# The down product of a bilinear gated unit, on one Trainium2 core: eight block products replaced by seven over 1024 tokens

## The chip, the core and the metric

The kernel is one program on one NeuronCore of a Trainium2 chip. The metric is the device time of one execution in microseconds (us). Engines are called by the profile's names: PE (TensorE, matmuls), PEld (its weight loads), DVE (VectorE), ACT (ScalarE), POOL (GpSimd) and SP (SyncE, which issues most DMAs). Each engine works through its own instructions strictly in the order in which the kernel was written, and waits at an instruction until what it reads and overwrites is free; so the order on each engine is as important as the amount of work.

## The reference

Cut to the part that the change touches. Sizes: S = 2048 tokens, D = 640, F = 1536, one batch, float32.

```python
x = A_u
sa, ca, ga, sb, cb, gb = ...                 # six rows of D from silu(c) @ w_mod
h = layernorm(x) * (1 + ca) + sa
x = x + ga * long_convolution(h, ...)        # the first two thirds of the time
h = layernorm(x) * (1 + cb) + sb
g = h @ w_gate                               # D -> F
u = h @ w_up                                 # D -> F
x = x + gb * ((g * u) @ w_down)              # F -> D: the down product
```

## The kernel before

The convolution fills the first 530 us or so of the span and is left as it is. Then comes the gated unit, in two halves of 1024 tokens, each of two blocks of 512 tokens. Every half has a stage that makes g * u for twelve blocks of 128 of F (the up stage), and a stage that multiplies it by w_down (the down stage).

**Precision by splitting.** A float32 product is made of three faster ones: each operand is split into hi and lo (`hilo`, L1020: ACT writes hi, DVE subtracts to get lo), and PE adds up hi x hi, lo x hi and hi x lo (`prod`, L1053). So every operand that PE reads costs one ACT and one DVE instruction first. Both are recorded under the helper's lines: L229 for ACT, L1022 for DVE.

**The up stage** (loop over f, L1565 on) makes, for each block f of F, products `y_1`, `z_1`, `y_2`, `y_3`, `z_2` (and `x_1`, `x_2` for a block three steps ahead); DVE adds them out of PSUM (L1394 in `y_1`, L1406 in `y_2`, L1425 in `y_3`, L1414 in `z_2`), multiplies for the first token block (L1419), and POOL adds and multiplies for the second (L1408, L1426). The results are tiles `a` of 128 x 512: the transposed g * u, by block of F. The products lie in six PSUM banks used in turn (`pa`, L1061), so a product can start only when the sum that was made six products earlier has been read out.

**The down stage** (L1606 on) runs over token blocks T and over f. `d_prep` (L1431) splits one tile `a` (512 columns) and one block of 128 rows of w_down (640 columns, tiles wga, wsgh, wsgl); `down` (L1446) then runs 24 matmuls: 4 groups of 128 tokens x 3 products x 2 column ranges, 384 and 256 wide. That is 48 steps in all, 24 for each half, 1152 matmuls. `d_prep` runs three steps ahead (LEAD). After twelve steps `fin` (L1467) adds the sum to the residual x on DVE (L1471, L1474) and stores it. w_down is multiplied by gb on POOL during the first up stage (`fold`, L1491, product at L1503) and kept in a DRAM tile, wdg.

**What the first down stage carries besides.** The second half's tokens need a layer norm first: `stats` (L1509: 20 DVE statistics instructions, L1105, for each block, then a chain of short ones, L1091 and L277 to L284, with a square root on ACT between them), `head_i` (four ACT instructions of 640 columns), and `tokens2` (four PE transposes, an ACT scaling, a split). A table, LATER (L1519), says at which step each is written; before, they stand at steps 1 to 4 of the first token block and at steps 0 to 9 of the second.

## Time and profile before

| | us |
|---|---|
| runs | 1008.56, 1013.97, 1013.34 (median 1013.34) |
| span of the profiled execution | 1012.8 |
| first up stage until first down matmul | to 683.47 |
| first down stage until the second half's first product | 683.47 to 775.79 |
| second half's first products and up stage | 775.79 to 923.95 |
| second down stage | 923.95 to about 1008.6 |
| last sums and stores | to 1012.8 |

The profiled execution has a span of 1012.8 us; the device time of an execution adds what lies around its span, and the profile does not give it for this one. Stage borders are read in the timeline of PE. The profile is read by three things: the busy time of each engine in a stretch of time, what an engine waited for, and the timeline of one engine, where a square bracket behind a row gives the idle time before it and who ended it.

### The profile page before, as it was taken

The numbers are of one execution on the slowest core, as the hardware profiler recorded it, in microseconds if no ns is written. First come the engines' busy times: TensorE is split into PE (matmuls) and PEld (weight loads), VectorE is DVE, ScalarE is ACT, GpSimd is POOL, SyncE is SP. The second block draws the span as 40 slices with busy tenths as digits, with TensorE's granted clock in tenths as the row PEclk, the third lists the DMA queues.
The fourth block names the chain that finished last, engine by engine and source line by source line (L and its number), as shares of the span: only waits on it lengthen the run. The fifth ranks groups of instructions, "written<-read, shape, count | busy, mean of one in ns | idle before, by whom it ended". The sixth has DMA issues, their size and how long they took to land. (4 is left out here: it accounts for less than half of the span.)

```text
span 1012.8 us, 26818 instructions
## 1 busy us (share of the span) xinstructions
PE 897.8 (89%) x11192; PEld 732.0 (72%) x11192; DVE 765.8 (76%) x1389; ACT 574.4 (57%) x1049; POOL 572.4 (57%) x423
## 2 busy tenths in 40 slices
PE   4864798799789689988888999999999999999998
PEld 3653566576576467666746788889998888889998
DVE  8698578987989987893977977787576787768452
ACT  4759999987888897872437322234464422224331
POOL 4976899799869989950035576661112354452000
PEclk9876799999979989999999999999999999999999
DMA  7654665454445553558673444524644422221341
GB/s 243 236 140 151 235 230 151 161 163 130 142 129 159 168 150 104 179 170 283 209 208 94 151 134 136 191 109 130 211 157 160 152 79 82 86 67 54 103 157 52
DMA packets 147817, 153.16 MB, mean 151 GB/s; under 512 B 9200, under 2 KB 125424, under 8 KB 146288
## 3 DMA queue, kind: packets, MB, share of 16 engines
q1 hardware_dynamic: 145968, 148.43, 46.4%
q10 hardware_dynamic: 1728, 3.02, 0.8%
q8 instruction: 88, 1.44, 0.6%
...
HBM read 110.45 MB, written 40.96 MB: 150 GB/s over the span
## 5 line engine op out<-in xcount | busy, mean ns | idle before, releaser
L708 POOL TENSOR_TENSOR EQ<-LQ,RH 128x1536 f32<-128x1536 f32 x40 | 124.2, 3106 | 23.0 <-DVE QtB L765 22.8
L229 ACT ACTIVATE z<-pa 128x512 f32<-128x512 f32 x24 | 14.4, 599 | 168.6 <-PE pa L1057 120.5
L1022 DVE TENSOR_TENSOR wsgl<-wga,wsgh 128x640 fp32r<-128x640 f32 x72 | 67.9, 947 | 45.7 <-ACT wsgh L229 45.6
L229 ACT ACTIVATE wsgh<-wga 128x640 fp32r<-128x640 f32 x72 | 52.6, 732 | 66.7 <-PE pa L1459 42.7
L1408 POOL TENSOR_TENSOR z<-z,s 128x512 f32<-128x512 f32 x24 | 33.6, 1400 | 92.9 <-DVE s L1407 92.9
L1034 POOL TENSOR_TENSOR tf<-wur,wgb 128x256 f32<-128x256 f32 x24 | 18.9, 785 | 93.1 <-DVE wtl L1022 57.7
L1459 PE MATMUL pa<-wsgh,sh 128*128 128x384 f32 (+1 forms) x304 | 69.7, 310 | 0.0
L1459 PE MATMUL pa<-wsgl,sh 128*128 128x384 f32 (+1 forms) x304 | 69.2, 309 | 0.0
L1459 PE MATMUL pa<-wsgh,sl 128*128 128x384 f32 (+1 forms) x304 | 69.1, 309 | 0.0
L708 POOL TENSOR_TENSOR EP<-LP,RH 128x768 f32<-128x768 f32 x40 | 66.1, 1652 | 0.0
L708 POOL TENSOR_TENSOR Pha<-LH,DH 128x1536 int32<-128x1536 int32 (+1 forms) x21 | 62.5, 2974 | 3.7 <-ACT trb L229 3.3
L708 POOL TENSOR_TENSOR Phb<-LH,DH 128x1536 int32<-128x1536 int32 x20 | 62.3, 3115 | 3.1 <-ACT tra L229 3.1
L1022 DVE TENSOR_TENSOR wtl<-tf,wth 128x256 fp32r<-128x256 f32 (+1 forms) x72 | 60.1, 861 | 0.0
L820 PE MATMUL kg<-QtB,PtB 64*32 64x64 f32 x2560 | 48.2, 227 | 4.9 <-DVE QtB L764 4.9
L820 PEld LDWEIGHTS kg<-QtB,PtB 64*32 64x32 f32 x2560 | 41.0, 113 | 12.8 <-DVE QtB L764 6.2
L1406 DVE TENSOR_TENSOR s<-pa,s 128x512 f32<-128x512 f32 x24 | 16.6, 690 | 44.6 <-PE pa L1057 39.6
L1057 PE MATMUL pa<-sh,wtl 128*128 128x512 f32 x144 | 45.1, 395 | 4.2 <-DVE wtl L1022 4.2
L1459 PEld LDWEIGHTS pa<-wsgh,sh 128*128 128x128 f32 x304 | 46.6, 188 | 0.0
L1459 PEld LDWEIGHTS pa<-wsgh,sl 128*128 128x128 f32 x304 | 46.6, 188 | 0.0
L1459 PEld LDWEIGHTS pa<-wsgl,sh 128*128 128x128 f32 x304 | 46.6, 188 | 0.0
L1057 PE MATMUL pa<-sh,wth 128*128 128x512 f32 x144 | 44.7, 391 | 0.0
L1057 PE MATMUL pa<-sl,wth 128*128 128x512 f32 x144 | 44.5, 390 | 0.0
(576 smaller groups left out, 2953.2 us busy)
## 6 DMA issues: line engine op xcount, KB each, us to landing
...
```

The lines of the kernel that those rows point to most:

```text
L229: return S.activation(o, i, f, **kw)
L708: G.tensor_tensor(o.rearrange("p x (h l) -> p x h l", l=8), lo.unsqueeze(2).to_broadcast([P, rows, nh, 8]), hi.rearrange("p h x -> p x h") ...
L820: PE.matmul(kg[j * 32 : j * 32 + 32, dd, :], PtB[lo : lo + 64, c, r, :], QtB[lo : lo + 64, c, r, :], start=False, stop=dd == 7 and c == 1, ...
L1022: V.tensor_tensor(lo, v, hi, op=OP.subtract)
L1034: G.tensor_tensor(t[:, 0:2], u[:, 0:2], g[:, 0:2], op=OP.subtract)
L1057: PE.matmul(ps, w[a][:, k], x[b][:, l], start=n == 0 and m == 0, stop=n == 2 and m == len(ks) - 1)
L1406: V.tensor_tensor(S67[i], ps, S6[i], op=OP.add)
L1408: G.tensor_tensor(ZT[i], ZT[i], S67[i], op=OP.add)
L1459: PE.matmul(ACC[tb][t][c], x[:, ts], w[:, cs], start=st, stop=f == NF - 1 and n == 2 and (c == 0 or t % 2 == 1))
```

## The change

The down product of a half is now taken as one product of 1024 x 1536 by 1536 x 640, cut into 2 x 2 blocks on each side: tokens 512 and 512, F 768 and 768, D 320 and 320. Instead of the eight block products it makes seven (Winograd's form of Strassen's method), of sums and differences of blocks. A product runs over six blocks of F, two at a time, so it has three steps; a half has 21 steps q = 0 to 20, each with 24 matmuls of 320 columns (4 groups of 128 tokens x 2 blocks of F x 3 products), 1008 in all.

- The tiles `a` are held in pairs of two blocks of F, 128 x 1024 (`AV`; AV[0..5] first token block, AV[6..11] second). `d_prep(h, q)` splits one such pair (1024 columns) and one 128 x 640 tile of weights for each step, two steps ahead. In the first half the lo part of steps 8, 10, 12, 14 and 16 is made on POOL instead of DVE (`hilo` has an engine as argument).
- Block sums of the left side: `half_sum` (m = 0, 1, 2; written behind steps 0, 1, 2) is POOL add, DVE subtract, POOL subtract, each of 1024 columns (lines 1460, 1461, 1462 of the new kernel); `half_sum4` (behind steps 7, 8, 9) is a POOL subtract (line 1465). Sum and operands are read by steps 6 to 17.
- Block sums of w_down: `fold` in the first up stage keeps its twelve products with gb and adds twelve subtractions of 640 columns on POOL, and writes seven blocks for each part of F to wdg.
- Results: a product lies in four PSUM banks, two products in turn in eight banks. `fin` behind every third step adds a product to the residual blocks: product 0 is copied out by ACT (four copies of 320) and added on POOL, products 1 to 6 are added on DVE straight from PSUM (4 or 8 instructions of 320, line 1543), and the sums that several results share are added on POOL behind that (8 for product 2, 4 for product 5).
- The second half's token work moves: `stats` of both blocks is written in the last two steps of the first up stage, each behind `d_prep` of that step; `head_i` behind steps 1 and 2, the transposes behind steps 7, 10 and 13, the sums for the second up stage behind 15 and 16.

The diff, cut to its core:

```diff
+    DW, NP, NQ = D // 2, 7, 21
...
-        PAIRS += [("d", 2 * h + T, 2 * p) for T in range(2) for p in range(NF // 2)]
+        PAIRS += [("d", h, q) for q in range(0, NQ, 2)]
...
-    def hilo(hi, lo, v):
+    def hilo(hi, lo, v, e=None):
         act(hi, v)
-        V.tensor_tensor(lo, v, hi, op=OP.subtract)
+        (e or V).tensor_tensor(lo, v, hi, op=OP.subtract)
...
+    AHEAD = 4
+    PROD = (0, 3, 0, 6, 9, None, 3)
+    AH, WD2, AR, S1, XR, ACC, U = {}, {}, {}, {}, {}, {}, {}
...
+    def half_sum(h, m):
+
+        S1[m] = two(mk(("wth", "wth", "wtl")[m], [P, 8, P], F32R, 2).bitcast(F32))
+        x11, x21, x22 = AV[m], AV[6 + m], AV[9 + m]
+        G.tensor_tensor(S1[m], x21, x22, op=OP.add)
+        V.tensor_tensor(x21, x11, x21, op=OP.subtract)
+        G.tensor_tensor(x11, S1[m], x11, op=OP.subtract)
+
+    def half_sum4(h, m):
+        G.tensor_tensor(AV[3 + m], AV[3 + m], AV[m], op=OP.subtract)
+
+    def slot_of(q):
+
+        if q < 2:
+            if q == 0:
+                AR[0] = [mk(n, [P, NB, 512], F32R) for n in ("hh1", "hl1")]
+            return [t[:, 2 * q : 2 * q + 2] for t in AR[0]]
+        if q < 18:
+            if q == 2:
+                AR[0] = [mk(n, [P, 9, 512], F32R) for n in SX]
+            i = 2 * ((q - 2) % 4)
+            return [t[:, i : i + 2] for t in AR[0]]
+        return [two(mk(n, [P, 8, P], F32R, 2)) for n in ("wth", "wtl")]
+
+    def d_prep(h, q):
+
+        p, m = divmod(q, 3)
+        w = WR.pop(("d", h, q))
+        v = S1.pop(m) if PROD[p] is None else AV[PROD[p] + m]
+        if q < 20:
+            ah, al = slot_of(q)
+            hilo(ah, al, v, G if h == 0 and q in (8, 10, 12, 14, 16) else None)
...
+        WD2[h, q] = mk("wsgh", [P, D], F32R, 4), mk("wsgl", [P, D], F32R, 4)
+        hilo(*WD2[h, q], w)
+        if q % 2 or q == NQ - 1:
+            used(1)
...
+    def bank(p, t):
+        j = 4 * (p % 2) + t
+        return pa(ACC["b"] + j) if j < 6 else pg(j - 6)
+
+    def down(h, q):
+
+        p, m = divmod(q, 3)
+        if q == 0:
+            ACC["b"] = BANK[0]
+            BANK[0] += 4
+        if m == 0:
+            ACC[p] = [bank(p, t) for t in range(4)]
+        x, (dh, dl) = AH.pop((h, q)), WD2.pop((h, q))
+        last = h == 1 and q == NQ - 1
+        for a, b in [(t, j) for t in range(4) for j in range(2)] if last else [(t, j) for j in range(2) for t in range(4)]:
+            ts, ws = slice(a * P, a * P + P), slice(b * DW, b * DW + DW)
+            ah, al = x[b]
+            for n, (l, r) in enumerate(((ah, dh), (al, dh), (ah, dl))):
+                PE.matmul(ACC[p][a][:, :DW], l[:, ts], r[:, ws], start=m == 0 and b == 0 and n == 0, stop=m == 2 and b == 1 and n == 2)
...
+        def add(e, x, y):
+            for t in range(4):
+                e.tensor_tensor(x[t], y[t], x[t], op=OP.add)
+
+        if p == 0:
+            for t in range(4):
+                act(u[t], ps[t])
+            add(G, x11, u)
+        if p == 1:
+            add(V, x11, ps)
+            store(h, 0, 0)
+        if p == 2:
+            add(V, u, ps)
+            add(G, x21, u)
+            add(G, x22, u)
+        if p == 3:
+            add(V, x21, ps)
+            add(V, x22, ps)
+        if p == 4:
+            add(V, x21, ps)
+            store(h, 1, 0)
+        if p == 5:
+            add(V, u, ps)
+            add(V, x22, ps)
+            add(G, x12, u)
+            store(h, 1, 1)
+        if p == 6 and h == 0:
+            add(V, x12, ps)
+            store(h, 0, 1)
+        elif p == 6:
+            for t in range(4):
+                V.tensor_tensor(x12[t], ps[t], x12[t], op=OP.add)
+                (SY, S)[t % 2].dma_start(rows_of(h, 0, 1, outv)[:, t], x12[t])
...
+        if p < 2:
+            for k in ((0, 1, 2), (3,))[p]:
+                G.tensor_tensor(x[:, k], x[:, k], gbr, op=OP.mult)
+        if p == 1:
+            G.tensor_tensor(t1, b12, b11, op=OP.subtract)
+            G.tensor_tensor(t3, b22, b12, op=OP.subtract)
+        if p == 2:
+            G.tensor_tensor(t2, b22, t1, op=OP.subtract)
+            G.tensor_tensor(t4, b21, t2, op=OP.subtract)
+            rs = slice(2 * r, 2 * r + 2)
+            for c, b in ((0, b11), (1, b21), (6, b22)):
+                SY.dma_start(wdg[:, c, rs], b)
+            SY.dma_start(wdg[:, 2:6, rs].rearrange("p c j d -> p c (j d)"), FT[1])
+            if r < 2:
+                fold_l(r + 1)
...
+    LATER = {1: [(head_i, 2)], 2: [(head_i, 3)], 3: [(raw_u, NF)], 5: [(raw_u, NF + 1)],
+             7: [(new_h,)] + [(tokens2, 2, 0, k, False, (1, i)) for i, k in enumerate((0, 2, 1, 3))],
+             10: [(tokens2, 2, 0, 4, False, (0, 0))] + [(tokens2, 3, 1, k, False, (0, i + 1)) for i, k in enumerate((0, 2, 1))],
+             13: [(tokens2, 3, 1, 3, False, (1, 0)), (tokens2, 3, 1, 4, False, (1, 1))],
...
+    BOTH = {0: [(half_sum, 0), (res_l, 0, 0)], 1: [(half_sum, 1), (res_l, 1, 0)], 2: [(half_sum, 2)], 6: [(res_l, 1, 1)],
+            7: [(half_sum4, 0)], 8: [(half_sum4, 1)], 9: [(half_sum4, 2)], 15: [(res_l, 0, 1)]}
...
-                d_prep(2 * half, f - NF + 2)
-        for T in range(2):
-            tb = 2 * half + T
-            h2 = tb + 2 if half == 0 else None
-            for f in range(NF):
-                for n in (2, 3) if T == f == 0 else (f + LEAD,):
-                    if n < NF:
-                        d_prep(tb, n)
-                    elif T == 0:
-                        d_prep(tb + 1, n - NF)
-                    elif h2:
-                        split_g(n)
-                down(tb, f)
-                if f == NF - 1:
-                    fin(tb)
-                for g_, *a_ in LATER.get((T, f), ()) if h2 else ():
-                    g_(*a_)
+                d_prep(half, f - NF + 2)
+                if half == 0:
+                    for i_ in (0, 2):
+                        stats(f - NF + 4, i_)
+        for q in range(NQ):
+            if q + 2 < NQ:
+                d_prep(half, q + 2)
+            down(half, q)
+            if q % 3 == 2:
+                fin(half, q // 3)
+            for g_, *a_ in BOTH.get(q, ()):
+                g_(half, *a_)
+            for g_, *a_ in LATER.get(q, ()) if half == 0 else ():
+                g_(*a_)
```

**DVE, end of the first up stage.** Rows from the adds of the last-but-one block of F to the start of the down stage; `a`, `s`, `z`, `e` are the tiles of the up stage, `sl` or `hl` the lo part of a left operand, `wsgl` that of the weights. Before:

```order
L1022 TENSOR_TENSOR e<-a_7635,e 128x512
L1022 TENSOR_TENSOR wsgl<-wga,wsgh 128x640
L1394 TENSOR_TENSOR s_8894<-pa_8887,e 128x512
L1406 TENSOR_TENSOR s_8915<-pa_8908,s_8894 128x512
L1407 TENSOR_TENSOR s_8894<-z,s_8894 128x512
L1425 TENSOR_TENSOR s_8915<-pa_8919,s_8915 128x512
L1414 TENSOR_TENSOR s_8894<-pa_8931,s_8894 128x512
L1419 TENSOR_TENSOR a_8700<-a_8700,s_8894 128x512
L1022 TENSOR_TENSOR e<-a_7636,e 128x512
L1022 TENSOR_TENSOR wsgl<-wga,wsgh 128x640
L1022 TENSOR_TENSOR sl<-a_7637,sh 128x512
```

After (BN_STATS and what follows it are the layer norm's statistics):

```order
L1028 TENSOR_TENSOR hl_8889<-a_7630,hh_8888 128x1024
L1028 TENSOR_TENSOR wsgl<-wga,wsgh 128x640
L1111 BN_STATS st_8896<-xb_8814 128x6 x20
L1097 BN_AGGR mv_8917<-st_8896 128x2 x4
L277 TENSOR_SCALAR hr_8920<-mv_8917 128x4
L279 RECIPROCAL hr_8918<-hr_8921 128x4
L280 TENSOR_TENSOR hr_8921<-hr_8918 128x4
L281 TENSOR_TENSOR hr_8921<-hr_8921,hr_8920 128x4
L282 TENSOR_SCALAR hr_8921<-hr_8921 128x4
L283 TENSOR_TENSOR hr_8918<-hr_8918,hr_8921 128x4
L284 SCALAR_TENSOR_TENSOR hr_8919<-mv_8917,hr_8918 128x4
L1415 TENSOR_TENSOR s_8941<-pa_8934,e 128x512
```

The statistics of both token blocks now stand on DVE between the splits of steps 0, 1 and 2, the first of them ahead of the last block's adds out of PSUM, which begin with L1415 (L1394 of before).

**DVE, first steps of the down stage, after.** The rows from the split of step 2 on; L1461 is the middle instruction of `half_sum`:

```order
L1028 TENSOR_TENSOR sl<-a_7940,sh 128x1024
L1028 TENSOR_TENSOR wsgl<-wga,wsgh 128x640
L1461 TENSOR_TENSOR a_7635<-a_7630,a_7635 128x1024
L1028 TENSOR_TENSOR sl<-a_8162,sh 128x1024
L1028 TENSOR_TENSOR wsgl<-wga,wsgh 128x640
L1461 TENSOR_TENSOR a_8059<-a_7631,a_8059 128x1024
L1028 TENSOR_TENSOR sl<-a_8379,sh 128x1024
L1028 TENSOR_TENSOR wsgl<-wga,wsgh 128x640
L1461 TENSOR_TENSOR a_8282<-a_7940,a_8282 128x1024
L1028 TENSOR_TENSOR sl<-a_8602,sh 128x1024
L1028 TENSOR_TENSOR wsgl<-wga,wsgh 128x640
```

Each difference of blocks stands ahead of the split of the next step: L1461 for m = 2 is ahead of the split of step 5.

**POOL, the same place, after.** L1460 and L1462 are the first and last instruction of `half_sum`, L1543 the adds of product 0 to the residual:

```order
L1429 TENSOR_TENSOR z<-z,s_8962 128x512
L1447 TENSOR_TENSOR a_7636<-s_8962,z 128x512
L1460 TENSOR_TENSOR wth<-a_7635,a_8504 128x1024
L1462 TENSOR_TENSOR a_7630<-wth,a_7630 128x1024
L1460 TENSOR_TENSOR wth<-a_8059,a_8717 128x1024
L1462 TENSOR_TENSOR a_7631<-wth,a_7631 128x1024
L1543 TENSOR_TENSOR hh_9076<-s_9150,hh_9076 128x320
L1543 TENSOR_TENSOR hh_9076<-z,hh_9076 128x320
L1543 TENSOR_TENSOR hh_9076<-s_9152,hh_9076 128x320
L1543 TENSOR_TENSOR hh_9076<-tf,hh_9076 128x320
L1460 TENSOR_TENSOR wtl<-a_8282,a_7636 128x1024
L1462 TENSOR_TENSOR a_7940<-wtl,a_7940 128x1024
```

Before, POOL had nothing here between L1426 of the last block and the sums of weights for the second half. Now the first sum for m = 2 stands behind the four adds of product 0, and these need the end of step 2 on PE.

196 lines of the change are left out of this document (95 added, 101 removed).

## The prediction

> **What bounds the kernel now.** I read the page first: busy shares, then the chain that ended last.
>
> ```profile
> span 1012.8 us, 26818 instructions
> PE 897.8 (89%) x11192; PEld 732.0 (72%) x11192; DVE 765.8 (76%) x1389; ACT 574.4 (57%) x1049; POOL 572.4 (57%) x423
> PE 41%; DVE 1%; DMA 1%; POOL 1%; issue 1%; ACT 0%; DVEq 0%; SPq 0%; ACTq 0%
> ```
>
> An average over all stages says little, so the chain in order of time and the busy time by stretches come next: the second up and down stage are one unbroken run of matmuls in the chain, and in the windows PE is busy all of the time. 924 to 1008 us holds 576 matmuls, the whole second down stage.
>
> ```profile
> 775.79 148.33 PE pa L1057 x648
> 924.11 84.46 PE pa L1459 x576
> ```
> ```profile
> 683.00:725.00 42.00, 40.98 (x276) 40.33 (x275) 29.04 (x63) 19.89 (x32) 6.02 (x6) 1.00 0.48 150
> 924.00:966.00 42.00, 42.00 (x288) 42.00 (x287) 23.47 (x36) 16.05 (x27) 1.30 (x1) 1.00 0.32 96
> 966.00:1008.00 42.00, 42.00 (x288) 42.00 (x287) 15.90 (x27) 10.72 (x17) 0.00 (x0) 1.00 0.29 98
> ```
>
> The columns behind the stretch are PE, PEld, DVE, ACT and POOL, then the granted clock. DVE has 29.0 of 42 us in the first down stage, 23.5 and 15.9 in the second; POOL almost nothing. All that PE waited for from the first down stage until the second up stage:
>
> ```profile
> PE pa L1057 <- DVE xb L1471: 1.5, 1, 1.5
> PE pa L1459 <- DVE s L1414: 0.8, 1, 0.8
> PE pa L1459 <- DVE wsgl L1022: 0.2, 1, 0.2
> ```
>
> So both down stages are bound by PE, and before this change the other engines hide. What PE saves is gained only as far as PE is still never kept waiting.
>
> **What the change removes on PE.** 288 matmuls take 42.00 us, 0.146 us each for a mean of 320 columns, and 320 is the new width of all. Three matmuls of 512 columns start every 0.68 us:
>
> ```profile
> 605.36 0.84 PE L1057 MATMUL pa<-sh,wsuh 128*128 128x512 f32 x3
> 606.04 0.84 PE L1057 MATMUL pa<-sh,wsul 128*128 128x512 f32 x3
> ```
>
> That is 0.227 us for 512 and 0.146 for 320, a straight line with a small fixed part, so a new matmul is priced at 0.146. 1152 - 1008 = 144 matmuls go: 144 x 0.146 = **-21.0 us**, 10.5 in each half; a step is 24 x 0.146 = 3.5 us. The three waits above (2.5 us) belong to places that are rebuilt, so I take them off too and count the new waits in full: **-23.5**.
>
> **The end of the first up stage.** DVE before, last adds and first splits, and PE's start of the down stage:
>
> ```profile
> 680.02 0.68 DVE L1022 TENSOR_TENSOR e<-a,e 128x512 fp32r<-128x512 f32 x1
> 680.62 0.81 DVE L1022 TENSOR_TENSOR wsgl<-wga,wsgh 128x640 fp32r<-128x640 f32 x1
> 681.36 0.68 DVE L1394 TENSOR_TENSOR s<-pa,e 128x512 f32<-128x512 f32 x1
> 686.38 1.27 DVE L1419 TENSOR_TENSOR a<-a,s 128x512 f32<-128x512 f32 x1
> ```
> ```profile
> 683.47 0.75 PE L1459 MATMUL pa<-wsgh,e 128*128 128x384 f32 x4
> ```
>
> A split of 512 occupies DVE for 0.60 us (680.02 to 680.62) and one of 640 for 0.74, so 1024 columns cost about 1.16 and a whole split of a new step 1.9. The same place in the second half, where no fold stands beside it:
>
> ```profile
> 919.84 0.68 DVE L1394 TENSOR_TENSOR s<-pa,e 128x512 f32<-128x512 f32 x1
> 926.08 0.68 DVE L1022 TENSOR_TENSOR e<-a,e 128x512 fp32r<-128x512 f32 x1
> ```
> ```profile
> 923.95 0.75 PE L1459 MATMUL pa<-wsgh,e 128*128 128x384 f32 x4
> ```
>
> There DVE begins the last block's adds 4.1 us before the down stage (call its start T0) and the next split 6.2 us later, at T0 + 2.1. What is now written in between, in the first half, is the statistics:
>
> ```profile
> 694.48 2.02 DVE L1105 BATCH_NORM_STATS2 st<-xb 128x6 f32<-128x128 f32 x10
> 697.74 2.02 DVE L1105 BATCH_NORM_STATS2 st<-xb 128x6 f32<-128x128 f32 x10
> 699.68 0.72 DVE L1091 BATCH_NORM_AGGREGATE mv<-st 128x2 f32<-128x30 f32 x4
> 701.98 0.68 DVE L1022 TENSOR_TENSOR sl<-a,sh 128x512 fp32r<-128x512 f32 x1
> ```
>
> Two times 2.0 and the chain from 699.68 to 701.98: 6.3 us for a token block. Now the steps, counted from T0; where a price has two ends, the first is DVE or POOL alone, the second beside each other (rows below).
> - Step 0: the adds begin at -4.1 + 0.6 (wider split) + 6.3 = 2.8. PE's second group writes the bank that the first of them empties, so PE waits until 3.4 and ends step 0 at 6.4, not 3.5.
> - Step 1: its split begins 6.2 behind the adds, at 9.0, and its last part is done at 10.9 to 12.1. PE waits about 4 us and ends at 14.1 to 15.3.
> - Step 2: first the other block's statistics, 6.3, then the split, done at 19.1 to 20.3; PE waits about 4 more and ends at 22.3 to 23.5. ACT can't help: its hi part of step 2 stands behind the square root.
> - Steps 3 and 4: the POOL rows decide. Prices of POOL, and of DVE and POOL beside each other:
>
> ```profile
> 685.83 1.28 POOL L1426 TENSOR_TENSOR a<-s,z 128x512 f32<-128x512 f32 x1 [0.81 <-DVE s L1425]
> 667.78 0.74 DVE L1419 TENSOR_TENSOR a<-a,s 128x512 f32<-128x512 f32 x1
> ```
> ```profile
> L708 POOL TENSOR_TENSOR EP<-LP,RH 128x768 f32<-128x768 f32 x40 | 66.1, 1652 | 0.0
> ```
>
> No row has POOL at 1024 columns: twice 1.28 is 2.6, 1652 ns scaled by 1024/768 is 2.2, I take 2.4; 320 columns are 0.8. L1419 takes 0.74 us alone and 1.27 (686.38) while POOL's 1.28 runs. The first DVE difference is at 20.3 to 21.5; POOL then has two sums (4.8), DVE the second difference (1.2) and the split of step 4 (1.9, or 3.1 beside POOL): 28.2 to 30.6. PE ends step 4 at 31.4 to 33.8.
> - Step 5: behind the second difference (26.3 to 27.5) POOL has one sum (2.4), four adds of product 0 (3.2) and the first sum for m = 2 (2.4); then DVE the third difference (1.2) and the split of step 5 (1.9 to 3.1): 37.4 to 39.8. Only then is PE in step 5, which ends at 40.6 to 43.0; without waits, 21.0.
>
> So **20 us** are lost here (18, if POOL is at 2.2 and nothing slows, to 23). Ahead of step 12 the trace has transposes:
>
> ```profile
> 765.76 1.03 PE L1132 MATMUL psg<-ident,xb 128*128 128x128 f32 x8
> 766.55 0.54 PE L1459 MATMUL pa<-wsgh,hh 128*128 128x384 f32 x2
> ```
>
> - Step 12 (transposes stand behind step 10): product 2 needs 8 POOL adds (6.4), two block sums (4.8) and the lo part of step 12 (2.4), 14 us with the first DVE add, while PE has three steps and 16 transposes (eight take 0.8, first row to second), about 12: 2 lost, up to 7 beside DVE or if POOL starts late. I take **4**.
> - Second half, no statistics: split of step 1 done at 4.6 to 5.7, first difference at 7.7 to 8.8, POOL's two sums and the second difference at 13.7 to 14.8, then as above 2.4 + 3.2 + 2.4 + 1.2 + 1.9 to 3.1: step 5 is split at 24.8 to 27.1 and ends at 28.0 to 30.3, not 21.0. I take **8** (5 to 12).
>
> **Clock.** A wait costs more than its length if PE slows behind it:
>
> ```profile
> 469.74 1.06 PE L965 MATMUL psfa<-TVa,ct 64*32 64x512 f32 x8
> 477.14 2.66 PE L965 MATMUL psfa<-TVb,ct 64*32 64x512 f32 x8 [4.44 <-DMA TVb<-WD]
> ```
> ```profile
> 477.00:479.50 2.50, 2.36 (x8) 0.35 (x8) 0.00 (x0) 0.00 (x0) 0.00 (x0) 0.63 1.02 306
> 479.50:481.00 1.50, 1.50 (x14) 1.28 (x14) 1.16 (x3) 0.00 (x0) 0.00 (x0) 0.50 0.18 54
> ```
>
> Behind a wait of 4.44 us the granted clock was 0.63 and 0.50, and eight matmuls took 2.66 us instead of 1.06; with what follows at 0.50 some 2 us are lost. The waits ahead of step 5 in both halves and of step 12 are 4 to 6 us by the sums above and nothing hides what follows them: 0 to 6, I take **3**. (The Trainium skill, TensorE: Matmul & The Clock Gate, Part 1, puts the drop to half speed at an idle window of about 3.4 us. By it the waits ahead of steps 1 and 2 would count as well, an estimate of 1.7 us each and 3 in all, so 1028; but PE then waits for DVE anyway, and the trace has no wait between 1.5 and 4.4 us in these stages to decide it.)
>
> **At nothing.**
>
> ```profile
> L229 ACT ACTIVATE sh<-a 128x512 fp32r<-128x512 f32 x50 | 30.4, 618 | 4.6 <-PE pa L1057 4.6
> L1471 DVE TENSOR_TENSOR xb<-pa,xb 128x384 f32<-128x384 f32 x16 | 8.8, 547 | 9.8 <-PE pa L1459 9.8
> L1503 POOL TENSOR_TENSOR xb<-xb,gbr 128x640 f32<-128x640 f32 x12 | 21.3, 1798 | 0.0
> 560.00:683.00 123.00, 123.00 (x540) 100.95 (x539) 96.05 (x138) 34.76 (x80) 82.23 (x73) 1.00 0.43 142
> ```
>
> ACT's wider hi parts are hidden, since ACT had 19.9 of 42 us; uncovered, 0.6 us a step. DVE's adds from PSUM are narrower than L1471's 0.55 us; eight (4.4) and three splits (5.7) fit into a product's 10.5, so steps 6 to 11 hold. The twelve added POOL subtractions in the first up stage are some 12 x 1.8 = 22 us beside 82 of 123: hidden by PE's 123 of 123, and if DVE is slowed by them, it comes later to T0 by an us or two. SP's stores stand behind weight loads that were issued two steps earlier, and the smaller residual loads ahead of need. The transposes cost the same as before.
>
> **Sum.** -23.5 + 20 + 4 + 8 + 3 = +11.5 on a span of 1012.8: 1024.3. The median of the three runs lies 0.5 above that span, which gives **1025**. A difference under 0.5% (5 us) can't be told from none here.
>
> **Rivals.**
> - DVE on time (faster): DVE gets the last adds and the splits of steps 1 and 2 done as PE needs them, and the sums for m = 0 and 1 are over before step 2 ends. Then each half loses only the chain behind step 2, 0.4 + 3.2 + 2.4 + 1.2 + 1.9 = 9.1 against two steps, 7.0: 2. With step 12: -23.5 + 2 + 4 + 2 = -15.5, 998. For it: DVE has 13 of 42 us free in the old stage. Against: row 686.38, DVE is already 3 us behind T0 with its last multiplication. It decides if the split of step 1 ends before T0 + 3.5. Chance 0.16.
> - Lowest prices (no change): 18 + 2 + 5 and no slow clock: -23.5 + 25 = +1.5, 1015. POOL's 768-column row speaks for it. Chance 0.22.
> - Taking turns (slower still): DVE and POOL don't share but alternate on every instruction that reads two SBUF tiles. 686.38 fits: 0.55 us longer beside 0.7 us of POOL. Then from the first difference (21) on, 8 us of DVE (three splits, two differences) and 15 of POOL (five sums, four adds) add up and step 5 ends at 47: 26 lost, 12 in the second half, 7 at step 12, clock 6: +27.5, 1041. Chance 0.12. (The Trainium skill, GPSIMD Engine Reference, Key points, says that the two share their SBUF interfaces and names DVE instructions with two SBUF inputs; the L1419 rows agree that there is a price.)
> - PE saves less than the columns say: by the straight line 384 columns cost 0.173; if 320 cost halfway there, 0.160, 1008 x 0.014 = 14 us are missing, 1039. PEld is busy as long as PE in the windows, so a weight load as the bound is possible; the line speaks against it. Chance 0.04.
>
> **How the numbers follow.** The forecast, 1025, has what is left, 0.46. Slower by over 0.5%: 0.46 + 0.12 + 0.04 = 0.62; within: 0.22; faster: 0.16. The forecast's own range, 18 to 23, 2 to 7, 5 to 12 and 0 to 6, is 1015 to 1038. For 8 in 10 the range must take in the no-change case and part of the faster one: 1004 to 1037.
>
> **What would show it.** Right: in the first down stage PE has waits of 2 to 6 us for DVE at its steps 0, 1, 2 and 5, for POOL at step 12, and in the second at step 5; BN_STATS lies between the splits; the two stages hold 1008 matmuls at 0.146. Wrong: PE busy for all of both down stages (then 998 or less), POOL's 1024-column rows under 2.2 us, or waits at other steps, for DMA or ACT.

## The result, and the profile after

The changed kernel takes 1066.42 us (median of 4 runs, 1063.84 to 1068.54), the one before 1010.95 us in the runs beside it (4 runs, 1008.29 to 1013.97): a ratio of 1.0554, 95% interval 1.0509 to 1.0600. It is slower by over five per cent; 1025 was forecast, with a range of 1004 to 1037. The page of the changed kernel, the lines that the prediction began with:

```profile
span 1063.7 us, 26666 instructions
PE 896.1 (84%) x11048; PEld 724.2 (68%) x11048; DVE 856.9 (81%) x1412; ACT 586.5 (55%) x1047; POOL 700.3 (66%) x490
PE 26%; DVE 9%; POOL 7%; issue 3%; DMA 1%; ACT 1%; SPq 0%; DVEq 0%; POOLq 0%; ACTq 0%
```

PE does 144 matmuls less and is busy as long as before; DVE has 91 us more, POOL 128 us more, and both are in the chain that ended last. Where the time went is read stage by stage, from the first matmul of a stage to the first of the next. Busy time by windows, of the kernel before (first up, first down, second up, second down stage; PE, PEld, DVE, ACT, POOL, granted clock):

```profile
536.54:683.47 146.93, 142.71 (x622) 115.55 (x621) 117.73 (x167) 50.10 (x110) 96.73 (x83) 1.00 0.41 134
683.47:775.79 92.32, 89.77 (x618) 88.71 (x616) 65.84 (x140) 48.73 (x80) 17.09 (x15) 1.00 0.46 152
775.79:923.95 148.16, 148.16 (x648) 121.58 (x649) 111.13 (x166) 46.40 (x102) 64.29 (x63) 1.00 0.31 98
923.95:1008.60 84.65, 84.61 (x577) 84.41 (x575) 39.97 (x62) 26.82 (x44) 1.30 (x1) 1.00 0.30 98
```

The same four windows after the change:

```profile
530.93:684.84 153.91, 144.42 (x622) 115.03 (x621) 138.21 (x173) 47.51 (x106) 120.03 (x95) 1.00 0.46 152
684.84:813.83 128.99, 94.70 (x546) 90.36 (x545) 102.86 (x145) 54.95 (x78) 72.54 (x40) 0.87 0.32 100
813.83:969.32 155.49, 150.71 (x649) 123.36 (x649) 111.21 (x164) 48.91 (x106) 69.18 (x68) 0.98 0.24 73
969.32:1060.20 90.88, 79.41 (x505) 77.83 (x503) 74.25 (x78) 33.15 (x43) 45.54 (x27) 0.92 0.36 115
```

The first down stage is 36.7 us longer, the second 6.2, and the two up stages, where the matmuls are the same as before, 7.0 and 7.3. The first up stage begins 5.6 us earlier; that is ahead of everything the change touches, and in the profiles below, whose kernels are the same up to there, it begins anywhere from 524.6 to 536.9. So the stage lengths are compared, not the single spans. With 0.7 us less at the end that is 50.9, the difference of the two spans; the medians lie 55.5 apart, since the execution profiled before is one of the longer ones.

What PE waited for in these stages, largest first (line and tile, what it waited for, us in all, times, longest):

```profile
PE pa L1518 <- DVE wsgl L1028: 14.7, 11, 2.5
PE pa L1518 <- POOL sl L1028: 10.4, 2, 9.9
PE pa L1518 <- DVE sl L1028: 8.6, 4, 4.3
PE pa L1518 <- DVE hl L1028: 5.0, 2, 2.7
PE pa L1063 <- ACT hh L229: 4.8, 1, 4.8
PE pa L1518 <- DVE s L1415: 4.7, 1, 4.7
```

L1518 are the matmuls of the down stage; before, PE had three waits from the first down stage on, 2.5 us together. DVE's splits (`hl`, `sl`, `wsgl`) and one lo part on POOL now hold PE up. The timeline of DVE and POOL at the start of the first down stage (684.84, so called T0) shows how:

```profile
689.43 0.68 DVE L1415 TENSOR_TENSOR s<-pa,e 128x512 f32<-128x512 f32 x1
695.13 2.80 POOL L1460 TENSOR_TENSOR wth<-a,a 128x1024 f32<-128x1024 f32 x1
695.64 3.37 DVE L1028 TENSOR_TENSOR hl<-a,hh 128x1024 fp32r<-128x1024 f32 x1
705.82 1.22 DVE L1028 TENSOR_TENSOR sl<-a,sh 128x1024 fp32r<-128x1024 f32 x1
708.82 1.22 DVE L1028 TENSOR_TENSOR sl<-a,sh 128x1024 fp32r<-128x1024 f32 x1
708.99 3.30 POOL L1462 TENSOR_TENSOR a<-wth,a 128x1024 f32<-128x1024 f32 x1 [11.06 <-DVE a L1461]
709.96 3.01 DVE L1028 TENSOR_TENSOR wsgl<-wga,wsgh 128x640 fp32r<-128x640 f32 x1
712.25 2.98 POOL L1460 TENSOR_TENSOR wth<-a,a 128x1024 f32<-128x1024 f32 x1
723.70 2.37 POOL L1460 TENSOR_TENSOR wtl<-a,a 128x1024 f32<-128x1024 f32 x1
728.38 2.97 DVE L1028 TENSOR_TENSOR wsgl<-wga,wsgh 128x640 fp32r<-128x640 f32 x1
737.32 0.31 PE L1518 MATMUL pa<-wsgh,sh 128*128 128x320 f32 x1
```

Three things are to be seen. The last adds begin at 689.43, behind the statistics, as forecast, but at T0 + 4.6 and not at T0 + 2.8. A split of 1024 columns takes 1.22 us alone (705.82) and 3.37 beside a sum on POOL (695.64): it ends 1.1 us behind the end of POOL's instruction. And at 708.82 they go strictly in turn: DVE's split until 709.96, POOL's L1462 until 712.29, of which it needs 2.37 (what L1460 takes alone at 723.70), then DVE's `wsgl`, which was started at 709.96 and ends at 712.97, 0.7 behind POOL, then POOL's next sum. Step 6 begins at 737.32, T0 + 52.5; without waits it would be T0 + 21.

### The profile page after: what moved, and what is told of

Same layout as the page of the kernel before. It is cut to its first block, busy times and chain, and to the rows that moved or that the text cites. A ratio compares the mean times of both kernels' runs of the same rounds, so it can differ in the third digit from the quotient of the medians.

```text
span 1063.7 us, 26666 instructions
## 1 busy us (share of the span) xinstructions
PE 896.1 (84%) x11048; PEld 724.2 (68%) x11048; DVE 856.9 (81%) x1412; ACT 586.5 (55%) x1047; POOL 700.3 (66%) x490
## 5 line engine op out<-in xcount | busy, mean ns | idle before, releaser
L229 ACT ACTIVATE z<-pa 128x512 f32<-128x512 f32 (+1 forms) x26 | 15.2, 583 | 166.1 <-POOL a L1447 95.1
L1028 DVE TENSOR_TENSOR wsgl<-wga,wsgh 128x640 fp32r<-128x640 f32 x66 | 90.4, 1374 | 16.8 <-ACT wsgh L229 16.8
L1518 PE MATMUL pa<-wsgh,sl 128*128 128x320 f32 x184 | 59.6, 324 | 19.0 <-POOL sl L1028 10.4
L1028 DVE TENSOR_TENSOR wtl<-tf,wth 128x256 fp32r<-128x256 f32 (+1 forms) x72 | 71.0, 1011 | 0.0
L1518 PE MATMUL pa<-wsgl,sh 128*128 128x320 f32 x184 | 60.1, 327 | 11.5 <-DVE wsgl L1028 11.5
L1518 PE MATMUL pa<-wsgh,sh 128*128 128x320 f32 x184 | 59.0, 320 | 1.6 <-ACT wsgh L229 1.6
L1040 POOL TENSOR_TENSOR tf<-wur,wgb 128x256 f32<-128x256 f32 x24 | 19.8, 825 | 57.8 <-DVE wtl L1028 47.3
L229 ACT ACTIVATE sh<-a 128x1024 fp32r<-128x1024 f32 (+1 forms) x40 | 35.5, 902 | 35.8 <-POOL a L1462 19.7
L1518 PEld LDWEIGHTS pa<-wsgh,sl 128*128 128x128 f32 x184 | 36.5, 198 | 20.5 <-POOL sl L1028 10.9
L1028 DVE TENSOR_TENSOR sl<-a,sh 128x1024 fp32r<-128x1024 f32 (+1 forms) x36 | 48.0, 1348 | 3.0 <-ACT sh L229 3.0
L1518 PEld LDWEIGHTS pa<-wsgl,sh 128*128 128x128 f32 x184 | 36.6, 199 | 13.3 <-DVE wsgl L1028 13.3
```

What stands on the lines that cost most here:

```text
L229: return S.activation(o, i, f, **kw)
L1028: (e or V).tensor_tensor(lo, v, hi, op=OP.subtract)
L1040: G.tensor_tensor(t[:, 0:2], u[:, 0:2], g[:, 0:2], op=OP.subtract)
L1518: PE.matmul(ACC[p][a][:, :DW], l[:, ts], r[:, ws], start=m == 0 and b == 0 and n == 0, stop=m == 2 and b == 1 and n == 2)
```

## The experiments

Two theories stood against each other at first. **Turns:** while POOL works on an instruction that reads two SBUF tiles, DVE's instructions of that kind stand still, so that every sum on POOL costs DVE twice what DVE would need for it. **Room:** DVE simply has more work than fits, wherever it stands and whoever shares it. All kernels but the first and the last two of the table are the changed kernel with one edit or more; stage lengths in us, each from a profile of its own. Each ratio is to the kernel before in runs beside those of the row (medians of 1007.19 to 1012.01 us). A stage that an edit leaves alone still differs from profile to profile, by 0.5 us in the first up stage and by up to 1.2 in the others.

| kernel | time (ratio to before, interval) | up 1 | down 1 | up 2 | down 2 |
|---|---|---|---|---|---|
| before | 1010.95 | 146.9 | 92.3 | 148.2 | 84.6 |
| changed | 1066.42 (1.0554, 1.0509 to 1.0600) | 153.9 | 129.0 | 155.5 | 90.9 |
| statistics moved back | 1062.61 (1.0521, 1.0472 to 1.0571) | 153.5 | 126.8 | 154.5 | 90.6 |
| one block of them moved back | 1064.56, one run | 153.8 | 124.6 | 155.5 | 90.8 |
| sums on DVE | 1042.82 (1.0338, 1.0289 to 1.0387) | 153.8 | 115.5 | 155.6 | 82.3 |
| one input on POOL | 1053.96, one run | 153.9 | 125.3 | 155.5 | 88.1 |
| everything off POOL | 1038.56 (1.0267, 1.0223 to 1.0312) | 153.9 | 107.5 | 155.6 | 81.9 |
| filled wait, step 12 | 1065.11, one run | 153.8 | 126.4 | 154.7 | 90.4 |
| filled waits, all | 1058.04 (1.0499, 1.0430 to 1.0569) | 153.4 | 124.1 | 154.4 | 89.3 |
| fold on DVE | 1062.49, one run | 152.2 | 128.4 | 154.8 | 90.5 |
| load ahead of the fold's stores | 1060.21, one run | 151.0 | 128.4 | 154.8 | 90.5 |
| next sums behind block 5 | 1065.09, one run | 153.9 | 128.2 | 151.8 | 91.0 |
| what helped, together | 1027.26 (1.0174, 1.0136 to 1.0211) | 152.4 | 104.9 | 151.9 | 81.9 |
| seven products in the second half only | 1014.06 (1.0021, 0.9994 to 1.0049) | 146.9 | 92.3 | 148.2 | 87.0 |
| the same, mended | 1008.04 (0.9964, 0.9944 to 0.9985) | 146.9 | 92.3 | 148.2 | 81.5 |

**Statistics moved back.**

```diff
-                if half == 0:
-                    for i_ in (0, 2):
-                        stats(f - NF + 4, i_)
...
-    LATER = {1: [(head_i, 2)], 2: [(head_i, 3)], 3: [(raw_u, NF)], 5: [(raw_u, NF + 1)],
+    LATER = {3: [(raw_u, NF)], 5: [(raw_u, NF + 1), (stats, 2, 0)], 6: [(stats, 2, 2), (head_i, 2)], 8: [(stats, 3, 0)], 9: [(stats, 3, 2), (head_i, 3)],
```

> The statistics of the second rows go from the end of the first up stage to steps 5, 6, 8 and 9 of the first down stage, their normalisation behind them. Theory (order on DVE): steps 0 to 2 of the first down stage then go as in the second half, 15 us instead of 26, and the stage shrinks from 129 to about 118 us; time 1055 instead of 1066, up to 1060 if the 12.6 us of statistics hold back later splits. Rival (DVE has too much work in the stage wherever it stands, 103 of 129 us busy): what is gained ahead of step 3 is lost again between steps 6 and 14, the stage stays above 125 and the time above 1062.

Steps 0 to 2 did shrink, from 26.3 to 17.9 us, but the stage only from 129.0 to 126.8. PE's rows behind steps 7 and 10 (L1150 are the transposes of the second rows):

```profile
740.02 0.48 PE L1150 MATMUL pa<-ident,xb 128*128 128x128 f32 x1 [5.48 <-ACT xb L229]
768.51 0.48 PE L1150 MATMUL pa<-ident,xb 128*128 128x128 f32 x1 [11.11 <-ACT xb L229]
```

They wait for ACT's normalisation, and that for the statistics, which DVE came to late. The rival came in: the stage stays above 125 and the time above 1062. DVE has no room for the statistics in steps 5 to 9 either. Moving one block alone:

```diff
-    LATER = {1: [(head_i, 2)], 2: [(head_i, 3)], 3: [(raw_u, NF)], 5: [(raw_u, NF + 1)],
+    LATER = {1: [(head_i, 2)], 3: [(raw_u, NF)], 5: [(raw_u, NF + 1), (stats, 3, 0)], 6: [(stats, 3, 2)], 8: [(head_i, 3)],
...
-                    for i_ in (0, 2):
+                    for i_ in (0, 2) if f == NF - 2 else ():
```

> Only the second statistics block (token block 3) goes to steps 5 and 6 of the first down stage, and its normalisation to step 8; the first stays at the end of the up stage. Theory (each block of statistics in front of a split costs its 6.3 us once): step 2 goes from 10.4 + 4.8 us for steps 1 and 2 to about 8 together, 7 us less ahead of step 3; since the transposes of block 3 come only behind step 10, nothing waits for it there; the stage 129 to 122 and the time 1059. Rival (DVE has no room in steps 5 to 9): the transposes behind step 10 or the splits of steps 8 to 12 wait longer by what was gained, stage above 127.

7.4 us were gained up to the end of step 4, as much as expected but later: only 2.1 of them ahead of step 3. 4.6 went again at step 9, behind ACT's normalisation. 124.6 lies between the two.

**Sums on DVE.**

```diff
-        G.tensor_tensor(S1[m], x21, x22, op=OP.add)
+        V.tensor_tensor(S1[m], x21, x22, op=OP.add)
...
-        G.tensor_tensor(x11, S1[m], x11, op=OP.subtract)
+        V.tensor_tensor(x11, S1[m], x11, op=OP.subtract)
...
-        G.tensor_tensor(AV[3 + m], AV[3 + m], AV[m], op=OP.subtract)
+        V.tensor_tensor(AV[3 + m], AV[3 + m], AV[m], op=OP.subtract)
```

> All block sums (first and last instruction of each, and the later ones for product 6) are computed by DVE instead of POOL. Theory (while POOL reads two SBUF tiles, DVE's instructions of that kind stand still until it is done, so 2.4 us on POOL cost DVE more than the 1.2 us that it needs itself): the splits beside them go from 3.4 and 3.0 us back to 1.2 and 0.8, steps 1, 4 and 5 of the second half lose 1 to 5 us together instead of 16.9, the first half as much, and the wait ahead of step 12 goes from 9.9 to under 5; time 1041 (1034 to 1048). Rival (DVE is simply the fullest engine, and 18 instructions of 1.2 us more make it later): 1066 or more, with the waits of PE in the same places and longer.

1042.82, as "turns" had it; 24 us are gone, and DVE does 18 instructions more. The second half did not quite get there: its steps 1, 4 and 5 still lose 6.7 us, where 1 to 5 were expected. Both down stages, by windows:

```profile
678.37:793.87 115.50, 93.13 (x546) 88.84 (x545) 102.34 (x153) 54.96 (x78) 50.09 (x31) 0.87 0.36 111
949.43:1031.70 82.27, 77.48 (x505) 75.45 (x503) 75.00 (x87) 33.39 (x43) 22.70 (x18) 0.98 0.39 128
```

DVE's busy time in the first stage is 102.3 us where it was 102.9 in the changed kernel: 8 instructions more in the window, and not busier, because what counted as busy there was in good part standing. The edit changes two things at once, though: DVE no longer stands, and each sum takes 1.2 us on DVE instead of 2.4 or more on POOL. How the 24 us divide between the two is not shown. The waits left in it are mainly those behind the statistics, one of 4.9 us at step 12 and one of 3.6 at step 4.

**One input on POOL.** The second block is left out of both of POOL's sums, so that they read one tile.

```diff
-        G.tensor_tensor(S1[m], x21, x22, op=OP.add)
+        G.tensor_scalar(S1[m], x21, 1.0, None, op0=OP.mult)
...
-        G.tensor_tensor(x11, S1[m], x11, op=OP.subtract)
+        G.tensor_scalar(x11, S1[m], 1.0, None, op0=OP.mult)
```

> The two POOL instructions of each block sum read one SBUF tile instead of two (a multiplication by 1 of the same width; the second block is left out of the sum). It tells what makes DVE stand still. First theory (POOL must have two inputs): DVE's splits beside them take 1.2 and 0.8 us instead of 3.4 and 3.0, steps 1 and 4 of the second half lose nothing, time about 1050. Second theory (any POOL instruction on SBUF stops DVE's instructions with two SBUF inputs): a split of 1024 columns beside such an instruction still takes its own 1.2 us and nearly the whole of POOL's duration; the time falls only as far as POOL's duration does, by twice three times that. Rival of both (they share by rate): DVE's instruction is longer by half of the overlap or less.

The timeline of DVE and POOL in the second half (972.71 is an instruction without a neighbour; L1465, at the end, is a sum that the edit leaves at two tiles):

```profile
962.67 3.22 POOL L1460 TENSOR_SCALAR wth<-a 128x1024 f32<-128x1024 f32 x1
963.18 2.05 DVE L1028 TENSOR_TENSOR hl<-a,hh 128x1024 fp32r<-128x1024 f32 x1
970.03 1.65 DVE L1028 TENSOR_TENSOR wsgl<-wga,wsgh 128x640 fp32r<-128x640 f32 x1
972.71 2.77 POOL L1460 TENSOR_SCALAR wth<-a 128x1024 f32<-128x1024 f32 x1
991.55 2.37 POOL L1465 TENSOR_TENSOR a<-a,a 128x1024 f32<-128x1024 f32 x1
991.59 3.02 DVE L1028 TENSOR_TENSOR wsgl<-wga,wsgh 128x640 fp32r<-128x640 f32 x1
```

The split takes 2.05 us, neither 1.2 nor 3.4: it is 0.8 longer and runs beside POOL, whose instruction is 0.4 longer. The third theory, of shared rate, holds for one input on POOL; with two they take turns. The same kernel has both: the split of weights takes 1.65 us beside POOL's one-input instructions (970.03) and 3.02 beside L1465 (991.59), where it ends 0.7 behind POOL. In the stage lengths one input is worth 3.7 and 2.8 us, less than the sums on DVE (13.5 and 8.6), which take POOL's own time away as well; the rest of the lower time is an up stage that begins 5.1 us earlier.

**Everything off POOL.** As in sums on DVE, and:

```diff
-            hilo(ah, al, v, G if h == 0 and q in (8, 10, 12, 14, 16) else None)
+            hilo(ah, al, v, None)
...
-            add(G, x11, u)
+            add(V, x11, ps)
...
-    BOTH = {0: [(half_sum, 0), (res_l, 0, 0)], 1: [(half_sum, 1), (res_l, 1, 0)], 2: [(half_sum, 2)],
+    BOTH = {0: [(res_l, 0, 0)], 1: [(res_l, 1, 0)], 2: [(half_sum, 0)], 3: [(half_sum, 1)], 5: [(half_sum, 2)],
```

The other adds of products 2 and 5 go from `G` to `V` too, and still read `u`.

> All block sums, the lo parts of steps 8 to 16, and the adds of products 0, 2 and 5 go from POOL to DVE (those of product 0 straight from PSUM), and the block sums are written behind steps 2, 3 and 5 instead of 0, 1 and 2. Theory (POOL's two-tile instructions hold DVE up for longer than DVE needs for the same work, and the sums stand ahead of splits that are due earlier): the second down stage goes from 91 to 75 to 80 us, since DVE has some 1.6 us a step to spare there; the first one loses the 10 to 12 us at step 12 and 10 to 15 at steps 3 to 5 but keeps what the statistics cost (steps 0 to 2), 95 to 103 us instead of 129; time 1022 (1014 to 1032). Rival (DVE's total work bounds both stages once POOL helps no more): second stage over 85 and first over 115, time over 1040.

Steps 3 to 5 of the first half now lose 1.4 us together and step 12 nothing; but the expected 1022 was too low, and both stages (107.5 and 81.9) are above their ranges. Steps 0 to 2 still take 25.6, and steps 5 to 11 lose a little each, since DVE now does all of it. Here "room" is right: with POOL out of the way, DVE's own work is the bound of the first half. DVE is busy for 99.0 of its 107.5 us, and of PE's 18.4 us of waits 15.4 are for DVE.

**Filled waits.** PE multiplies old operands into accumulators that are overwritten, ahead of step 12 (64 matmuls), then ahead of all steps with long waits.

```diff
+        if h == 0 and q == 12:
+            for _ in range(16):
+                for t in range(4):
+                    PE.matmul(ACC[p][t][:, :DW], OLD[0][0][0][0][:, t * P : t * P + P], OLD[0][1][0][:, :DW], start=True, stop=True)
```

> Ahead of step 12 of the first half PE does 64 matmuls of 320 columns on the operands of step 11 into the accumulators that step 12 overwrites, 9.4 us, in the place of the 9.9 us wait. Theory (the slow matmuls behind a wait are the clock, 0.267 instead of 0.147 us each, granted 0.5): steps 12 and 13 take together 17 to 18 us instead of 20.1, every matmul starts 0.147 us behind the one before and the granted clock is 1.00 throughout; 2 to 3 us less in all, about 1063. Rival (they are slow since DVE and POOL load SBUF at that moment): 0.267 us apart in the same place, 20.1 us, no change.

The fillers took 9.4 us, step 12 then 4.5 and step 13 4.3, in the place of 20.1: 18.2 together, at a granted clock of 1.00 in every window from 752 to 784. So the slow matmuls behind a wait are the clock. By their spacing in the changed kernel,

```profile
694.33 0.47 PE L1518 MATMUL pa<-wsgh,hh 128*128 128x320 f32 x1
694.60 0.47 PE L1518 MATMUL pa<-wsgh,hl 128*128 128x320 f32 x1
```

0.27 us instead of 0.147, 126 matmuls of the two down stages are slow (0.20 to 0.27 us behind the one before), and what they take beyond 0.147 comes to 14.7 us. (The 22 us in the next expectation come out only if all gaps under 1 us are counted, and short waits are among those.) Whether that is all lost, the second kernel tells:

```diff
...
+    OLD, FILL = {}, ({0: 32, 1: 20, 2: 14, 3: 9, 4: 24, 5: 37, 12: 64, 20: 18}, {1: 18, 4: 16, 5: 44})
...
```

> The changed kernel with matmuls on old operands into idle accumulators ahead of the steps where PE waited (first half: 32, 20, 14, 9, 24, 37, 64 and 18 ahead of steps 0 to 5, 12 and 20; second half: 18, 16 and 44 ahead of steps 1, 4 and 5), about as many as fit into each wait; all other instructions stay. Theory (of the 22 us by which both down stages are longer than work and waits together, all is matmuls at half rate behind waits, so that full rate throughout gives most of it back, as far as DVE and POOL, which set the waits' ends, let it): granted clock 1.00 in both stages, first stage 129 to 113 to 119 us, second 91 to 85 to 88; time 1045 to 1053. Rival (DVE and POOL set the end of every step anyway, so that faster matmuls only wait longer): granted clock 1.00, but stages of 125 and 89 or more and 1060 or more.

The two down stages by windows, the first from its first filler (which stands ahead of step 0) on:

```profile
679.75:803.83 124.08, 115.67 (x764) 111.75 (x763) 99.16 (x141) 55.09 (x78) 71.95 (x40) 0.99 0.34 104
958.21:1047.50 89.29, 86.61 (x583) 85.26 (x581) 74.29 (x78) 33.15 (x43) 45.73 (x27) 1.00 0.37 117
```

At a clock of 0.99 and 1.00 the stages are 4.9 and 1.6 us shorter, 6.5 in all, not 22: the rival is nearer, though the time, 1058.04, is under its 1060. Of the 14.7 us at half rate some 8 are covered: the next split was not done yet anyway. The fillers were not too long where it counts: behind those of step 5 in both halves and of step 12 PE still has to wait.

**The up stages.** Three kernels ask why these are longer. The fold's block differences on DVE:

```diff
-            G.tensor_tensor(t1, b12, b11, op=OP.subtract)
+            V.tensor_tensor(t1, b12, b11, op=OP.subtract)
```

(and so t2, t3 and t4)

> The twelve added subtractions of the fold in the first up stage are done by DVE instead of POOL. Theory (each takes POOL 1.8 us, in which DVE's splits stand; DVE itself would need 0.74): the first up stage, from its first matmul to that of the down stage, goes from 153.9 to 147 to 150 us (146.9 in the kernel before), and the waits of 1.77 and 1.99 us in it go; time 4 to 6 us less, about 1061. Rival (the stage is longer for another reason, its buffers or its stores): 153 to 156 us, no change.

152.2, no more than 1.7 of the 7.0. The other cause is in SP's queue; a timeline of the changed kernel, SP, ACT and PE:

```profile
582.47 1.65 SPq L1618 DMA_DIRECT2D wdg<-xb  x3
590.07 0.36 SPq L1619 DMA_DIRECT2D wdg<-xb  x1
592.12 1.35 SPq L1001 DMA_DIRECT2D wga<-B_w_gate  x1
602.82 0.74 ACT L229 ACTIVATE wsgh<-wga 128x640 fp32r<-128x640 f32 x1 [14.01 <-DMA wga<-B_w_gate]
604.89 0.73 PE L1063 MATMUL pa<-sh,wth 128*128 128x512 f32 x2 [1.77 <-ACT wth L229]
```

The fold's last store (L1619) waits for POOL's differences until 590; the next gate weights stand behind it, ACT waits for them 14 us, and PE for ACT.

```diff
...
+            if r == 0:
+                raw()
+                SKIP.append(1)
             for c, b in ((0, b11), (1, b21), (6, b22)):
                 SY.dma_start(wdg[:, c, rs], b)
```

> In the first round of the fold the load of the next gate weights is issued ahead of the fold's four stores instead of behind them. Theory (those stores wait for POOL's subtractions, and the load behind them in SP's queue goes out at 592 instead of 582 us): the wait of 1.77 + 0.58 us in the first up stage goes, the stage 153.9 to 151 us. Rival (POOL's load on DVE is what delays the weights there): no change, 153 to 154.

151.0: the wait is gone, 2.9 of the 7.0 us. The other 2.4 us, if the two add up, were not taken apart. For the second up stage, POOL's and PE's rows of the changed kernel:

```profile
830.74 1.33 POOL L1040 TENSOR_TENSOR tf<-wur,wgb 128x256 f32<-128x256 f32 x1 [20.27 <-DVE wtl L1028]
834.51 1.25 POOL L1406 TENSOR_TENSOR s<-xb,xb 128x512 f32<-128x512 f32 x1
837.00 1.31 PE L1063 MATMUL pa<-hh,wth 128*128 128x512 f32 x2 [4.78 <-ACT hh L229]
```

The difference of the fifth block (L1406) stands behind four sums of weights (the first is L1040) that are needed later.

```diff
             split_u(i0, "c")
-            sums_u(i0 + 1)
...
             for k in (2, 3):
                 s_one(k)
+            sums_u(i0 + 1)
```

> At the start of the second up stage the four POOL instructions that sum the next weights are written behind the difference of the fifth block of U instead of ahead of it. Theory (these 4 instructions, 830.7 to 834.5, are what PE waits for in its 4.78 us): the wait goes to about 1, and with the clock behind it the stage from 155.7 to 150 us; time about 1061. Rival (the chain begins earlier, at a DMA and ACT's copies, and the next weights come too late instead): a wait of 3 us or more stays or comes back at the next weights, 154 us or more.

151.8 us, two waits of 1.36 and 0.63 in the place of 4.78; the theory holds, 2 us short. The other 3.6 of the 7.3 us stay open.

**What helped, together.** Everything off POOL, one block of statistics moved back, and the two reorderings of the up stages.

> The changed kernel with all that helped put together: everything off POOL and the block sums behind steps 2, 3 and 5, the difference of the fifth block ahead of the next sums of weights, the statistics of token block 3 in steps 5 and 6, and the first fold's load of up weights ahead of its stores. Theory (each loss has its own place): first down stage about 103, second up stage 151 to 152, second down stage 84 to 86, first up stage 151 to 152; time 1027 to 1033. Rival (DVE without POOL has no room for the statistics in steps 5 to 9): the first down stage stays at 107 or is longer, time 1034 to 1040.

1027.26 and the stages about as expected (the second down stage, 81.9, even below): each loss has its own place. But this is still 1.7% slower than before, for the first half's 104.9 us. Step 20 alone takes 8.9 of these instead of 3.5. In the changed kernel it takes 8.4: PE waits 0.8 and 2.0 us for DVE's last splits, which run beside POOL's sums of the next weights, and then runs at half rate. No kernel here moves those sums.

**Seven products in the second half only.** This is the kernel before; its first half is untouched. The seven-product stage of everything off POOL follows the second up stage, and the sums of the folded weights are made there.

```diff
+            else:
+                fold2(f)
...
+        if half:
+            for q in range(NQ):
+                for n in (2, 3) if q == 0 else (q + LEAD,):
+                    if n < NQ:
+                        d_prep2(n)
+                down2(q)
+                if q % 3 == 2:
+                    fin2(q // 3)
+                for g_, *a_ in BOTH.get(q, ()):
+                    g_(*a_)
+            break
```

> The kernel before, with seven block products only for the second 1024 rows' half (token blocks 2 and 3): the first half, its statistics, transposes and its fold are the ones of before, the sums of weights are made by DVE in the second up stage, all block sums and adds by DVE, those for m = 0, 1, 2 behind steps 0, 2 and 4, splits three steps ahead, and the sums for product 6 behind steps 11 to 13. Theory (DVE has the room in the second half, 13 of 42 us free at the start and 26 later, and none in the first): 10.5 us less of PE in the second down stage, 2 to 4 lost at steps 1 to 8, 0 to 2 in the up stage; 1003 to 1008 beside 1010 to 1012 of the kernel before. Rival (any form of seven products loses more than it saves, since the sums have to be done somewhere): 1011 or more.

No difference from before that can be told. Its second down stage takes 87.0 us, and step 1 alone 10.1: DVE has two sums of weights (L1538 is the first) just ahead of the last adds, so that the splits of step 1 are late; PE waits 2.4 and 0.9 us for them and runs at half clock behind that (0.50 from 934 to 937.8). ACT waits long for the weights of step 2. From the timeline of DVE, PE and ACT:

```profile
919.96 0.81 DVE L1538 TENSOR_TENSOR xb<-xb,xb 128x640 f32<-128x640 f32 x1
930.45 0.41 PE L1606 MATMUL pa<-wsgh,hl 128*128 128x320 f32 x1 [2.37 <-DVE hl L1027]
935.05 0.74 ACT L229 ACTIVATE wsgh<-wga 128x640 fp32r<-128x640 f32 x1 [10.12 <-DMA wga<-wdg]
```

These weights stood in SP's queue behind the loads of the residual rows. That held ACT up, but PE has no wait at step 2 (3.6 us), so step 1 is not long for it. In the next kernel those loads follow behind steps 0 and 1, and the sums of weights are done earlier:

```diff
-        r, p = divmod(f, 4)
+        r, p = divmod(f, 3)
...
-    BOTH = {0: [(half_sum, 0)], 2: [(half_sum, 1)], 4: [(half_sum, 2)], 11: [(half_sum4, 0)], 12: [(half_sum4, 1)], 13: [(half_sum4, 2)]}
+    BOTH = {0: [(res_l, 2, 0)], 1: [(res_l, 3, 1), (half_sum, 0)], 2: [(half_sum, 1)], 4: [(half_sum, 2)], 11: [(half_sum4, 0)], 12: [(half_sum4, 1)], 13: [(half_sum4, 2)]}
```

> The kernel with seven products in the second half only, with three things moved: the sums of weights are done two blocks of F earlier in the second up stage, the residual rows are loaded behind steps 0 and 1 instead of ahead of the down weights, and the block sum for m = 0 stands behind step 1 instead of 0. Theory (its second down stage lost 12.4 us of 10.5 + 1.9 saved: 6.5 at step 1, where ACT waited 10.1 us for weights that stood behind the residual's load in SP's queue and DVE had 1.65 us of weight sums ahead of the last adds, and 3.7 at step 6): step 1 loses under 2 us, step 6 under 3, the second down stage 78 to 81 us to its last matmul instead of 86.6; 1005 to 1009, 0.3 to 0.7 % under the kernel before. Rival (the losses only move on to later steps, since DVE's work is what fills the stage): 85 us or more and no difference from the kernel before.

```profile
921.64:1003.10 81.46, 76.73 (x505) 73.95 (x503) 76.22 (x134) 34.56 (x61) 1.86 (x2) 1.00 0.37 129
```

81.5 us, 3.2 less than the kernel before, at a clock of 1.00. Steps 1 and 6 lose 1.5 and 2.1 us, as expected; which of the three moves did it is not shown. 1008.04 us beside 1009.53 for the kernel before (medians of 12 and 17 runs), a ratio of 0.9964 (0.9944 to 0.9985). It is the one version that is faster than the kernel before, by a third of a per cent, and the interval only just excludes no difference. PE is busy for 76.7 and DVE for 76.2 of the 81.5 us, and of PE's 4.6 us of waits 4.2 are for DVE's splits: there is little room left on either.

## Why the prediction was wrong, step by step

The terms of its sum, with what the profile after has in their place (us; step ends as start times of the next step's first matmul):

| term | forecast | measured |
|---|---|---|
| matmuls saved, old waits gone | -23.5 | -21.1 and -2.5 |
| first half, steps 0 to 5 | +20 (18 to 23) | +31.4 |
| first half, step 12 | +4 (2 to 7) | +12.3 |
| first half, other steps | 0 | +6.1 |
| second half | +8 (5 to 12) | +16.8 |
| clock | +3 (0 to 6) | in the rows above; 6.5 by filled waits |
| first up stage | 0 | +7.0 |
| second up stage | 0 | +7.3 |
| ahead of and behind the stages | 0 | -6.3 |

They add up to 51.0, the spans differ by 50.9. The -6.3 is chance and no part of the mechanism: 5.6 of it is the earlier begin of the first up stage. Without it the miss would have been larger. Point by point:

- **PE's saving was right.** Fourteen steps in a row of the second half take 3.52 us each, 0.147 a matmul; the rival of a dearer matmul is out. So is the rival that DVE is on time.
- **The order on DVE was right in kind.** Waits stand at steps 0 to 5 and 12 of the first half and 1, 4 and 5 of the second, and mostly for what was named; a wait at step 20 of the first half was not foreseen and makes up 4.8 of the 6.1 us in "other steps". Without the statistics steps 0 to 2 were 8.4 us shorter.
- **The step that failed: "where a price has two ends, the first is DVE or POOL alone, the second beside each other".** It let DVE and POOL slow each other while both run; the runs show that one stands still for as long as the other's instruction takes. The upper end for a split was 3.1 us; beside a sum it takes 4.2 (1.2 and 3.0, rows 708.82 and 709.96), POOL's sum 3.3 and not 2.4. That shared pace was read off one row, L1419 at 1.27 beside POOL's 1.28, which fits taking turns as well: POOL ends at 687.11, DVE 0.54 later. The rival of taking turns had the mechanism, with a chance of 0.12: it put 8 us of DVE and 15 of POOL in a row from T0 + 21 on. They began at T0 + 24.0 (708.82) and the split of step 5 was done at 731.35, 22.5 us later, T0 + 46.5. The forecast had allowed 17 to 18 us from the first difference to that point; it took 23.7, so some 6 of the 11.4 us by which this term was short lie there. About 3 were there before step 3 (at T0 + 26.3 instead of 22.3 to 23.5), and the matmuls of step 5 took 6.0 us at half rate and not 3.2. Even that rival's 1041 is 25 us short, 14.3 of them in the up stages, which it had at nothing as well. (The Trainium skill, GPSIMD Engine Reference, Key points, names the shared SBUF interfaces; these rows agree with it, and put the price at the whole length of POOL's instruction where that has two inputs.)
- **Step 12** failed in the same way. Product 2's eight adds took POOL 10.2 us instead of 6.4 beside DVE's splits, the two sums 5.2 and the lo part 3.0. From the timeline of POOL, DVE and PE:

```profile
765.25 5.24 POOL L1465 TENSOR_TENSOR a<-a,a 128x1024 f32<-128x1024 f32 x2
765.89 0.88 DVE L1543 TENSOR_TENSOR hl<-pa,hl 128x320 f32<-128x320 f32 x2
770.45 6.22 POOL L1028 TENSOR_TENSOR sl<-a,sh 128x1024 fp32r<-128x1024 f32 x2
773.42 0.63 PE L1518 MATMUL pa<-wsgh,sl 128*128 128x320 f32 x1 [9.91 <-POOL sl L1028]
```

- **"At nothing" was wrong for both up stages.** The fold's subtractions were hidden by PE's busy time, it said, and SP's stores by loads issued earlier. That was said of the down stage's loads. In the first up stage the store stands ahead of a load and waits for POOL; in the second, POOL's sums stand ahead of a difference that PE needs. Undone singly, the queue, the subtractions and the sums give 2.9, 1.7 and 3.7 of 14.3 us; the other 6.0 stay open.
- **The clock** was too small a term by the count of slow matmuls (14.7 us) and about right by what filling the waits gave back (6.5). (The Trainium skill, TensorE: Matmul & The Clock Gate, Part 1, speaks of a free-running window of about 3.4 us; the rows agree with the free running. In the second half PE waits 2.29 and 0.32 us at step 1, and the clock is 0.50 from 977 to 979; it waits 2.31 at step 4, and the clock stays at 1.00. Each stretch at half clock in the two down stages lasts 3.4, 6.8 or 10.2 us.)

So the forecast had the sign and most of the places, and missed by 41 us even with an early begin that took 6 off: it took two engines that work in turn as sharing, it did not walk through two queues in the up stages, and it had a first half whose DVE had no room left.
